# Loads of chunks 2 to 4, of x's last two groups and of the inverse table, issued from GpSimd's queue instead of SyncE's

## The chip, the cores and the metric

The kernel runs on one core of a Trainium2 chip. A core has five engines that run their own instruction streams: PE (TensorE, matrix multiplications, written as a weight load PEld and a matmul PE), DVE (VectorE), ACT (ScalarE), POOL (GpSimd) and SP (SyncE, which here only issues transfers). Sixteen DMA engines move data between the chip's memory (DRAM) and the on-chip memory; a transfer is issued by an instruction on SP, ACT or POOL and runs by itself after that. Engines wait for each other, and for transfers, through semaphores. The metric is the device time of one execution in microseconds (us), as the median of several.

## The reference

Two branches are added to the input x = A_q (2048 positions, 640 channels, bf16), both fed with the layer-normalised xn:

```python
x = A_q
xn = _layernorm(x, axis=-1)
# A: a short 4-tap shift of k, times v, a long causal convolution by FFT, gated by xn
k_shift = sum(k_pad[:, t:t + S, :] * shift_k[:, ks - 1 - t] for t in range(ks))
kv = k_shift * v
y = irfft(rfft(kv, padded to 2S) * rfft(ssm_k, padded to 2S))[:S] + kv * ssm_D
A = xn * y
# B: a gated feed-forward layer
B = (sigmoid(xn @ w_gate) * (xn @ w_up)) @ w_down
return x + A + B
```

S is 2048, the hidden size of B is 1728.

## The kernel before

Positions are laid out as 128 partitions x 16 blocks, so `x[:, b, :]` is block b of every partition.

*Branch B* goes through four groups t of four blocks each (512 positions). Group t is normalised on DVE (statistics `st` L198, `mv`, `var` L210), its `rstd` is a power on POOL (`ln_pow`, L214), `xn` is written by DVE (L219), TensorE transposes it (`pt`, L234), ACT copies it to `xnT`. Then 13 pairs of gate and up products (`pg`, `pu`, L257) follow, ACT's sigmoid, DVE's multiplication into `hT` (L272), and the down product `pd` (L301), which DVE adds to x (L306). x's group 0 is loaded at the start, groups 1 to 3 later (`load_x`, L129). The four buffers of the pool `psG` hold these products; whatever DVE or ACT has not emptied keeps TensorE back.

*Branch A* goes through five chunks c of 128 channels. Each chunk needs these loads: the taps `sraw` (`load_taps`, L143), the channel weights `dr` and the filter `hn` (`load_h`, L136 and four times L139), `kx` (a halo of two transfers, L159 and L160, and two halves, L155), and `kvh` with v (two halves, L169). ACT turns `sraw` into `sc` (`taps`, L151). DVE transposes `hn` into the second half of `kvh` (`h_turn`, L320), POOL adds `dr` to one row of it (`add_D`, L314), DVE makes kv in 16 steps (`kv_op`, L334 to L343). TensorE makes the first transform step (`ps1`, L360 and L362), ACT copies it to `t1` (L223), SP writes that to DRAM (`wr1`, L374) and reads it back in another order (`rd2`, L384); a second transform step, a product, the inverse steps with a second trip through DRAM (`wr2` L438 and L442, `rdb` L452) and the multiplication with xn follow. `t1` has two buffers: ACT's third copy waits until the first write is down. `kx` has two buffers, one for even and one for odd chunks, `kvh` has two, `hn`, `sraw`, `sc` and `dr` one each.

Tables are loaded once: `S1t` for the forward transform, `TBt` for the last inverse step (first used at 143.7 us).

The order of all work is written out by hand in the string `ORDER`: each letter takes the next step of one chain, and the program's order on every engine follows from it. `m` are the early loads in one row (weights, chunks 0 and 1, x's group 1), `n` are x's groups 2 and 3 and then `TBt`; `h`, `K`, `V` and `T` are the loads of `hn`, `kx`, `kvh` and `sraw` for the later chunks; `H`, `D` and `k` are `h_turn`, `add_D` and `kv_op`; `P` is `ln_pow`; `w` and `r` are `wr1` and `rd2`. Every engine works strictly in its own order, so an instruction that waits holds back all that stand behind it on the same engine. In the kernel before, all transfers but three at the start stand in SP's order, about 160 instructions long. Each transfer in a queue also waits, by the way semaphores are given out, for the eighth transfer before it.

Of the kernel before, what the change touches and what calls it, by code (L numbers as in the profile page):

```python
# [19 lines left out]
P = 128  # L20
NB = S // P
# [36 lines left out]
def kernel(  # L58
# [14 lines left out]
    nc = tc.nc  # L73
    xr = A_q.flatten_outer_dims().rearrange("(p b) d -> p b d", b=NB)
    kr = A_k.flatten_outer_dims().rearrange("(p b) d -> p b d", b=NB)
    vr = A_v.flatten_outer_dims().rearrange("(p b) d -> p b d", b=NB)
# [3 lines left out]
    Drow = A_ssm_D.rearrange("(o d) -> o d", o=1)  # L80

    s1bits, tbbits, smbits = _tables()
    srow = A_shift_k.rearrange("d m -> (d m)").rearrange("(o n) -> o n", o=1)
    S1d = nc.inline_tensor(s1bits, name="tabS1")
    TBd = nc.inline_tensor(tbbits, name="tabTB")
# [4 lines left out]
    dr = ctx.enter_context(tc.tile_pool(name="dr", bufs=1, space=bass.MemoryType.DRAM))  # L90
# [8 lines left out]
    TBt = res.tile([P, 2, NB, P], U16, name="TBt")  # L99
# [12 lines left out]
    kxs = [res.tile([P, NB + 3, P], BF16, name="kx%d" % i) for i in range(2)]  # L112
# [8 lines left out]
    sync = nc.sync  # L121
# [3 lines left out]
    cin = [dict() for _ in range(NC)]  # L125

    def load_x(eng, g, n=4):
        for b in range(4 * g, 4 * g + 4, n):
            eng.dma_start(x[:, b:b + n, :], xr[:, b:b + n, :])  # L129

    def load_h(c):

        d = cin[c]
        d["hn"] = cv.tile([P, 4, 512], BF16, name="hn")
        d["dr"] = cv.tile([1, P], BF16, name="dr")
        sync.dma_start(d["dr"][:, :], Drow[:, c * P:(c + 1) * P])  # L136
        for q in range(4):
            src = A_ssm_k[c * P:(c + 1) * P, 512 * q:512 * q + 512].rearrange("(k r) t -> r k t", k=4)
            sync.dma_start(d["hn"][32 * q:32 * q + 32, :, :], src)  # L139

    def load_taps(c):
        cin[c]["sraw"] = cv.tile([P, 4 * P], BF16, name="sraw")
        sync.dma_start(cin[c]["sraw"][:], srow[:, 4 * c * P:4 * (c + 1) * P].to_broadcast((P, 4 * P)))  # L143

    def taps(c):
        sc = cv.tile([P, 4, P], BF16, name="sc")
# [5 lines left out]
        cin[c]["sc"] = sc  # L152

    def load_k(c, lo, hi):
        sync.dma_start(kxs[c % 2][:, lo + 3:hi + 3, :], kr[:, lo:hi, c * P:(c + 1) * P])  # L155

    def load_halo(c):
        cs = slice(c * P, (c + 1) * P)
        sync.dma_start(kxs[c % 2][16:P, 0:3, :], kr[15:P - 1, NB - 3:NB, cs])  # L159
        sync.dma_start(kxs[c % 2][1:16, 0:3, :], kr[0:15, NB - 3:NB, cs])  # L160

    def slot(c):

        if "kvh" not in cin[c]:
            cin[c]["kvh"] = cv.tile([P, 2, NB, P], BF16, name="kvh", bufs=2)
        return cin[c]["kvh"]

    def load_v(c, lo, hi):
        sync.dma_start(slot(c)[:, 0, lo:hi, :], vr[:, lo:hi, c * P:(c + 1) * P])  # L169

    def load_w(eng, lo, hi, u):
        if u == 0:
# [345 lines left out]
    def step(k, fn, *args):  # L518
        chains[k].append((fn, args))
# [16 lines left out]
    def hs(c):  # L536
        return [(load_h, c)]

    def ks(c):
        return [(load_halo, c), (load_k, c, 0, 8), (load_k, c, 8, NB)]  # L540

    def vs(c):
        return [(load_v, c, 0, 8), (load_v, c, 8, NB)]

    for k in ((load_w, sync, 512, 768, 0),
              (load_w, sync, 512, 768, 1),
              (load_taps, 0),
              (sync.dma_start, SMt[:], SMd.ap()),
              (load_w, sync, 768, 1024, 0),
              (load_w, sync, 768, 1024, 1),  # L550
              (load_w, sync, 1024, 1280, 0),
              (load_w, sync, 1024, 1280, 1),
              (load_wd, sync, 0, 7),
              *ks(0),
              (load_w, sync, 1280, FF, 0),
              (load_w, sync, 1280, FF, 1),
              *hs(0),
              *vs(0),
              (load_wd, sync, 7, NFC),
              (sync.dma_start, S1t[:], S1d.ap()),  # L560
              *hs(1),
              (load_x, sync, 1),
              *ks(1),
              *vs(1)):
        step("m", *k)
    for k in ((load_x, sync, 2), (load_x, sync, 3), (sync.dma_start, TBt[:], TBd.ap())):
        step("n", *k)
    step("Z", taps, 0)

    for c in range(NC):  # L570
# [28 lines left out]
        if c == 0:  # L599
            continue  # L600
        step("T", load_taps, c)
        step("t", taps, c)
        if c > 1:
# [70 lines left out]
```

## Time and profile before

| | us |
|---|---|
| median of 3 runs (239.5 to 239.63) | 239.56 |
| the profiled execution | 240.16 |
| its span | 238.4 |
| PE busy | 232.6 (98%) |
| DVE busy | 190.5 (80%) |
| ACT busy | 140.9 (59%) |
| POOL busy, 24 instructions | 11.2 (5%) |

The profile is one execution. A busy time is the time in which an engine had an instruction running; issuing a transfer is not counted. In lines of the timeline the columns are: start in us, length in us, engine, line of the kernel, operation, written tile <- read tile, and at the end in brackets the idle time before it and what ended that. In the chain of work that ended last each line is a start, a length and what the time went to. A tile's own answer gives, for each line, the shortest, median and longest duration in ns and the first and last start. SPq and ACTq are the issues of transfers on SP and ACT; the length of such a line is that of the issue, not of the transfer.

### The profile page before, as it was taken

The page shows a single profiled execution, that of the slowest core. Times are in us where ns is not written, and L with a number is a line of the kernel's source. Part 1 is how long each engine was busy: PE and PEld are TensorE (multiplying, and loading weights), DVE is VectorE, ACT ScalarE, POOL GpSimd, SP SyncE. Part 2 cuts the span into 40 slices and gives each one's busy share as a digit, 9 for nine tenths or more (in the row PEclk, how much of TensorE's full clock was granted, in tenths as well). Part 3 has the DMA queues.
Part 4 walks back from the last instruction along what each step waited for, and adds up shares of the span by engine and source line. Part 5 has one row for each costly group of instructions (what it writes and reads, how often), then busy time and mean ns, then how long its engine had stood idle before and what let it go on. Part 6 is the DMA issues. An engine that isn't in the chain of part 4 may idle for free.

```text
span 238.4 us, 5555 instructions
## 1 busy us (share of the span) xinstructions
PE 232.6 (98%) x2265; PEld 134.8 (57%) x2265; DVE 190.5 (80%) x350; ACT 140.9 (59%) x178; POOL 11.2 (5%) x24
## 2 busy tenths in 40 slices
PE   8899999999999999999999999999999999999994
PEld 2664445877555555667754434577664434456772
DVE  4633989999999999999999999865585695968372
ACT  2343322728557898764888787997558858764000
POOL 5210000020000000002000000000000000000000
PEclk9999999999999999999999999999999999999999
DMA  7999999998998999998444889875849795285494
GB/s 213 291 315 236 254 326 294 197 257 236 251 312 252 259 292 292 297 252 313 154 179 143 235 237 265 216 231 202 230 119 223 186 282 126 83 241 145 123 303 137
DMA packets 89119, 54.82 MB, mean 230 GB/s; under 512 B 47814, under 2 KB 83206, under 8 KB 88838
## 3 DMA queue, kind: packets, MB, share of 16 engines
q1 hardware_dynamic: 88150, 53.66, 81.3%
q10 hardware_dynamic: 944, 0.82, 1.1%
q8 instruction: 17, 0.28, 0.5%
q14 instruction: 8, 0.07, 0.1%
HBM read 36.12 MB, written 18.35 MB: 228 GB/s over the span
## 4 chain that ended last, share of the span: by engine, by line
PE 91%; DMA 5%; ACT 2%; issue 0%; ACTq 0%; DVE 0%
PE pd L301 26%; PE pg L257 22%; PE pu L257 22%; PE psb L461 4%; PE ps L360 3%; PE ps L362 3%; PE ps L393 3%; DMA w<-in_B_w_up_dram 3%; PE psa L422 2%; PE pg L278 2%; PE pt L234 2%; DMA d<-t 2%; ACT t L223 1%; PE pu L248 1%; PE pg L248 1%
## 5 line engine op out<-in xcount | busy, mean ns | idle before, releaser
L257 PEld LDWEIGHTS <-w 128*128 128x128 bf16 x500 | 46.4, 98 | 54.4 <-issue 5.3
L301 PE MATMUL pd<-wd,hT 128*128 128x320 bf16 (+2 forms) x448 | 64.3, 299 | 0.0
L257 PE MATMUL pg<-xnT,w 128*128 128x512 bf16 x250 | 62.2, 379 | 0.0
L257 PE MATMUL pu<-xnT,w 128*128 128x512 bf16 x250 | 62.2, 379 | 0.0
L301 PEld LDWEIGHTS <-hT 128*128 128x128 bf16 x448 | 42.3, 98 | 18.5 <-issue 1.7
L266 ACT ACTIVATE sig<-pg 128x512 bf16<-128x512 f32 x52 | 31.3, 605 | 29.8 <-PE pg L257 28.0
L272 DVE TENSOR_TENSOR hT<-sig,pu 128x512 bf16<-128x512 bf16 x52 | 35.2, 680 | 15.5 <-PE pu L257 9.6
L223 ACT CAST t<-ps 128x1024 bf16<-128x1024 f32 x40 | 39.2, 1023 | 12.1 <-DMA d<-t 7.9
L223 ACT CAST xz<-ps 128x1024 bf16<-128x1024 f32 x40 | 38.5, 1017 | 10.6 <-PE ps L393 10.5
L306 DVE TENSOR_TENSOR x<-pd,x 128x320 bf16<-128x320 f32 (+2 forms) x32 | 15.3, 479 | 15.5 <-PE pd L301 15.3
L408 DVE TENSOR_TENSOR xz<-xz 128x2048 bf16<-128x2048 bf16 x20 | 24.3, 1217 | 0.2
L360 PE MATMUL ps<-kvh,S1t 128*128 128x128 bf16 x160 | 21.2, 217 | 0.5 <-ACT t L223 0.5
L362 PE MATMUL ps<-kvh,S1t 128*128 128x128 bf16 x160 | 21.2, 220 | 0.0
L340 DVE TENSOR_TENSOR acc<-acc,tmp 128x1024 bf16<-128x1024 bf16 x30 | 20.7, 689 | 0.6
L338 DVE TENSOR_TENSOR tmp<-kx,sc 128x1024 bf16<-128x1024 bf16 x30 | 20.5, 685 | 0.4
L223 ACT CAST ao<-psa 128x1024 bf16<-128x1024 f32 x16 | 15.6, 1014 | 6.0 <-PE psa L422 3.9
L362 PEld LDWEIGHTS <-S1t 128*128 128x128 bf16 x160 | 15.4, 96 | 2.9 <-issue 0.8
L466 DVE TENSOR_TENSOR yx<-psb,xn 128x512 bf16<-128x512 f32 x20 | 13.8, 690 | 3.9 <-PE psb L461 2.9
L360 PEld LDWEIGHTS <-S1t 128*128 128x128 bf16 x160 | 15.5, 97 | 2.3
L223 ACT COPY xnT<-pt 128x640 bf16<-128x640 bf16 x16 | 10.2, 708 | 10.9 <-PE pt L234 10.6
L198 DVE BATCH_NORM_STATS2 st<-x 128x6 f32<-128x320 bf16 x32 | 13.7, 470 | 2.6 <-DMA x<-in_A_q_dram 2.6
L406 DVE STREAM_SHUFFLE xz<-xz 128x512 f32<-128x512 f32 x20 | 14.5, 725 | 0.0
(44 smaller groups left out, 147.5 us busy)
## 6 DMA issues: line engine op xcount, KB each, us to landing
d<-t SPq DMA_DIRECT2D x20, 512.0 KB, 3.9
t<-d SPq DMA_DIRECT2D x20, 512.0 KB, 5.2
bi<-d SPq DMA_DIRECT2D x8, 512.0 KB, 5.2
d<-ao SPq DMA_DIRECT2D x6, 512.0 KB, 4.1
kx<-in_A_k_dram SPq DMA_DIRECT2D x10, 256.0 KB, 5.1
hn<-in_A_ssm_k_dram SPq DMA_DIRECT2D x20, 128.0 KB, 5.9
kvh<-in_A_v_dram SPq DMA_DIRECT2D x10, 256.0 KB, 5.3
x<-in_A_q_dram SPq DMA_DIRECT2D x3, 640.0 KB
```

The source lines that it names most:

```text
L223: nc.scalar.copy(out=out, in_=in_)
L257: nc.tensor.matmul(pg[:, :], lhsT=w[:, c, u * UP + fc * P:u * UP + (fc + 1) * P], rhs=xnT[:, :, c, :], start=(c == 0), stop=(c == NC - 1))
L266: nc.scalar.activation(sig[fc][:, :], pgs[0, fc][:, :], ACT.Sigmoid)
L272: nc.vector.tensor_tensor(hT[:, fc, :], sig[fc][:, :], pgs[1, fc][:, :], ALU.mult)
L301: nc.tensor.matmul(pd[:, :], lhsT=hT[:, fc, bb * P:(bb + 1) * P], rhs=wd[:, fc, es], start=(fc == 0), stop=(fc == NFC - 1))
L306: nc.vector.tensor_tensor(x[:, 4 * t + bb, es], pds[bb, half][:, :], x[:, 4 * t + bb, es], ALU.add)
L338: nc.vector.tensor_tensor(d["tmp"][:, :, :], kx[:, lo + 3 - m:hi + 3 - m, :], sb(m), ALU.mult)
L340: nc.vector.tensor_tensor(d["acc"][:, :, :], d["acc"][:, :, :], d["tmp"][:, :, :], ALU.add)
L360: nc.tensor.matmul(ps[:, i, 0:P], lhsT=S1[:, b, h, :], rhs=cin[c]["kvh"][:, 0, b, :], start=True, stop=True)
L362: nc.tensor.matmul(ps[:, i, P:2 * P], lhsT=S1[:, b, h, :], rhs=hp[:, b // 2, b % 2, :], start=True, stop=True)
L406: nc.vector.stream_shuffle(z[:, 2, :, :].bitcast(F32), z[:, 1, :, :].bitcast(F32), swap)
L408: nc.vector.tensor_tensor(z[:, 1:3, :, :], z[:, 0:1, :, :].to_broadcast((P, 2, 8, P)), z[:, 1:3, :, :], ALU.mult)
```

## The change

The loads of `dr`, `hn`, `sraw`, `kx` (halo and halves) and `kvh` take their queue from a new function: GpSimd for chunks 2, 3 and 4, SP for chunks 0 and 1. The three loads of chain `n` (x's groups 2 and 3, `TBt`) are issued by GpSimd too. `ORDER` is untouched, so these 39 issues keep their places in the program's order; they now stand in POOL's order, between its `add_D` and `ln_pow`, instead of in SP's. What stands on PE and DVE, and in which order, is the same.

```diff
+    def queue(c):
+        return nc.gpsimd if c > 1 else sync
+
     def load_h(c):
...
-        sync.dma_start(d["dr"][:, :], Drow[:, c * P:(c + 1) * P])
+        queue(c).dma_start(d["dr"][:, :], Drow[:, c * P:(c + 1) * P])
         for q in range(4):
             src = A_ssm_k[c * P:(c + 1) * P, 512 * q:512 * q + 512].rearrange("(k r) t -> r k t", k=4)
-            sync.dma_start(d["hn"][32 * q:32 * q + 32, :, :], src)
+            queue(c).dma_start(d["hn"][32 * q:32 * q + 32, :, :], src)
     def load_taps(c):
...
-        sync.dma_start(cin[c]["sraw"][:], srow[:, 4 * c * P:4 * (c + 1) * P].to_broadcast((P, 4 * P)))
+        queue(c).dma_start(cin[c]["sraw"][:], srow[:, 4 * c * P:4 * (c + 1) * P].to_broadcast((P, 4 * P)))
     def load_k(c, lo, hi):
-        sync.dma_start(kxs[c % 2][:, lo + 3:hi + 3, :], kr[:, lo:hi, c * P:(c + 1) * P])
+        queue(c).dma_start(kxs[c % 2][:, lo + 3:hi + 3, :], kr[:, lo:hi, c * P:(c + 1) * P])
     def load_halo(c):
         cs = slice(c * P, (c + 1) * P)
-        sync.dma_start(kxs[c % 2][16:P, 0:3, :], kr[15:P - 1, NB - 3:NB, cs])
-        sync.dma_start(kxs[c % 2][1:16, 0:3, :], kr[0:15, NB - 3:NB, cs])
+        queue(c).dma_start(kxs[c % 2][16:P, 0:3, :], kr[15:P - 1, NB - 3:NB, cs])
+        queue(c).dma_start(kxs[c % 2][1:16, 0:3, :], kr[0:15, NB - 3:NB, cs])
     def load_v(c, lo, hi):
-        sync.dma_start(slot(c)[:, 0, lo:hi, :], vr[:, lo:hi, c * P:(c + 1) * P])
+        queue(c).dma_start(slot(c)[:, 0, lo:hi, :], vr[:, lo:hi, c * P:(c + 1) * P])
...
-    for k in ((load_x, sync, 2), (load_x, sync, 3), (sync.dma_start, TBt[:], TBd.ap())):
+    for k in ((load_x, nc.gpsimd, 2), (load_x, nc.gpsimd, 3), (nc.gpsimd.dma_start, TBt[:], TBd.ap())):
         step("n", *k)
```

## The prediction

> **What bounds the kernel now.** I read the page's first part and its chain, then the table by stage, the waits, and last, in order of time, the queues of SP, POOL, DVE and PE between 40 and 120 us, where all the moved loads lie.
>
> The page's first part, for the whole span:
>
> ```profile
> PE 232.6 (98%) x2265; PEld 134.8 (57%) x2265; DVE 190.5 (80%) x350; ACT 140.9 (59%) x178; POOL 11.2 (5%) x24
> ```
>
> TensorE leaves 238.4 - 232.6 = 5.8 us. The table by stage says where, and where none is left (columns: stretch and length; busy us of PE, PEld, DVE, ACT, POOL with instructions; clock; DMA share; GB/s):
>
> ```profile
> 40.00:50.00 10.00, 10.00 (x103) 7.96 (x102) 9.77 (x21) 4.63 (x6) 0.43 (x1) 1.00 0.92 209
> 50.00:60.00 10.00, 10.00 (x95) 7.60 (x93) 9.86 (x20) 6.15 (x8) 1.75 (x2) 1.00 0.90 269
> 60.00:70.00 10.00, 10.00 (x62) 5.06 (x60) 9.74 (x17) 4.89 (x7) 0.00 (x0) 1.00 1.07 273
> 70.00:80.00 10.00, 9.51 (x93) 6.15 (x91) 9.51 (x15) 8.35 (x11) 0.42 (x1) 1.00 0.99 260
> 80.00:90.00 10.00, 10.00 (x93) 4.95 (x92) 9.86 (x18) 8.90 (x12) 0.00 (x0) 1.00 0.93 281
> 90.00:100.00 10.00, 10.00 (x102) 5.67 (x101) 9.63 (x15) 7.74 (x10) 0.42 (x1) 1.00 1.03 299
> 100.00:110.00 10.00, 10.00 (x110) 6.85 (x108) 9.73 (x26) 5.78 (x6) 1.10 (x1) 1.00 0.88 251
> ```
>
> TensorE is full in every stretch but one, which lacks 0.49 us. VectorE is nearly full as well, and so are the 16 DMA engines (0.88 to 1.07). POOL alone is free. The rest of the 5.8 us lies at the two ends, which the moved loads do not touch. The 0.49 us stands in the chain like this (start, us, what):
>
> ```profile
> 70.56 1.93 ACT t L223 x2
> 72.50 3.88 DMA d<-t
> 76.48 1.02 ACT t L223
> ...
> 77.55 0.22 PE ps L360
> ```
>
> A write of the first transform's output takes 3.88 us, ScalarE needs its buffer back, and TensorE waits for ScalarE. So the most that any change to the loads between 40 and 120 us can win is about 0.5 us, or 0.2%; losses have no such lid.
>
> **Part 1: what leaves SP.** 39 issues leave it: 12 for each of chunks 2 to 4 (dr 1, hn 4, sraw 1, kx 4, kvh 2), two of x, and TBt. Added from their rows in SP's timeline this is 23.6 us of issuing. It wins only where a write or read of the transform stood ready behind it. Two such places: the write at 46.23 (its copy ended about 45.66, from the row "43.74 2.87 ACT L223 x3"; SP was then waiting at sraw for ACT's sc) and the one at 49.22 (copy ended 48.02). The first can go 0.5 us earlier, the second 1.1; the write at 72.50 left 0.01 us after its copy and gains nothing from SP. Off the path: 0.
>
> **Part 2: what POOL gets.** The same 39 issues, in the same relative order, between its own add_D (L314) and rstd power (L214). Their price there is in no row. For a small one (dr, hn, sraw) the floor is SP's quickest issue, 0.26 us, the ceiling POOL's longest instruction of its own, 1.39 us; I take 1.0, nearer POOL's rows, since that engine does the work. For a quarter-megabyte kx or kvh load, 1,024 rows of 256 bytes, the nearest row is that load on SP (L155, min/median/max):
>
> ```profile
> L155 SPq DMA_DIRECT2D kx<-in_A_k_dram x10: 385/430/3021, 15.1 to 90.1; - x10
> ```
>
> Floor 0.39, ceiling 3.02, the latter from a queue that was backed up; I take the middle, 1.7. The Trainium skill, page "DMA: Bandwidth & Descriptors", section "Latency and other measured facts", puts the first byte of a load at about 1 us from GpSimd and 0.6 from SP; by that alone each load would land 0.4 us later, and the sum below would keep its sign.
>
> **Part 3: do the loads still land in time?** They wait for the same freed buffers as before, so they cannot start much earlier: sraw(3) and sraw(4) for ScalarE's sc (67.2, 84.8), with kx and kvh behind them; kvh(3) and kvh(4) for TensorE (about 75.9, 93.0), with add_D, x and rstd behind. Each load also waits for the eighth before it on its queue, long down at these prices. The question is POOL's backlog. These rows carry it, first POOL, then SP, VectorE and TensorE:
>
> ```profile
> 51.16 1.32 POOL L214 TENSOR_TENSOR rstd<-var,mhalf 128x4 f32<-128x4 f32 x1 [5.45 <-DVE var L210]
> 94.57 0.42 POOL L314 TENSOR_TENSOR kvh<-kvh,dr 1x128 bf16<-1x128 bf16 x1 [15.98 <-DVE kvh L320]
> ```
>
> ```profile
> 47.06 2.05 SPq L139 DMA_DIRECT2D hn<-in_A_ssm_k_dram  x4
> 93.10 1.13 SPq L169 DMA_DIRECT2D kvh<-in_A_v_dram  x2
> 96.23 0.42 SPq L129 DMA_DIRECT2D x<-in_A_q_dram  x1
> ```
>
> ```profile
> 56.40 2.10 DVE L320 STREAM_TRANSPOSE kvh<-hn 128x512 f32<-128x512 f32 x2
> 103.89 0.88 DVE L198 BATCH_NORM_STATS2 st<-x 128x6 f32<-128x320 bf16 x2
> 110.34 1.51 DVE L219 TENSOR_SCALAR xn<-x,mv,rstd 128x640 bf16<-128x640 bf16 x4
> ```
>
> ```profile
> 111.33 0.84 PE pt L234 x15
> ```
>
> *rstd of x's group 1.* It now stands behind dr(2) and hn(2)'s four loads, free when VectorE ends hn(1) at 46.2. At 1.0 each they end by 50.7, 0.4 us before rstd could start at 51.16: hidden. At the ceiling of 1.39 they end at 52.7, 1.5 late, and xn at 52.53 waits.
>
> *hn(2)* landed before at about 49.1 + 6.2 = 55.3; now 50.7 + 5.2 = 55.9 against 56.40: hidden, thinly. The kx and kvh loads of chunks 2 to 4 have 4 to 25 us until VectorE reads them (75.13 for kx(2)'s second half is the nearest).
>
> *x's group 2* is the pinch. Before: issued at 96.23; the longest landing of an x load is 7.0 us, so down at 103.2, used at 103.89. Now it stands behind both kvh(4) loads (buffer free at about 93.0) and add_D(4): 93.0 + 2 x 1.7 + 0.42 = 96.8, 0.6 us later, and with 0.4 for the dearer issue it is down at 104.2. VectorE stalls 0.3. TensorE's transposes begin at 111.33 with the first xn ready at 110.34 + 0.44 = 110.78: 0.55 us of cover, so 0 on the path. The cover is gone when the kvh load costs more than about 1.85 us.
>
> *x's group 3 and TBt* now wait behind the rstd of group 2 (done 110.3) instead of going at 107.0 and 107.6; used at 124.59 and 143.7: 0. *add_D(2 to 4)* wait behind kvh loads; TensorE reads their result 15 us later or more: 0.
>
> **Part 4: sharing.** With DMA at 0.9 to 1.07, what used to queue behind a write now runs beside it. At 46 us hn(2), 512 KB, stood behind the write of 46.23; at 209 GB/s it takes 2.5 us, and if half passes ahead the write lands 1.25 later, less the 0.5 of part 1: +0.75. ScalarE's copy at 52.75 waits for it; TensorE's next two groups, at 54.25 and 54.99, had 0.53 and 0.31 us in hand: +0.4. At 72.5 the write of 3.88 us shares with kx(3), issued on POOL at about 70 to 73.5 instead of by 70.8; half of 256 KB at 260 GB/s is 0.5: the wait of 0.49 becomes 1.0. Bounds: the first could cost nothing, the second could vanish (-0.49), or both take whole loads (+1.6, +1.0).
>
> **Sum.** 0 + 0 + 0 + 0.4 + 0.5 = +0.9 us. The profiled execution took 240.16 us (span 238.4), 0.6 above the median of 239.56; as a step it goes on the median: 240.5.
>
> **The rivals.**
>
> *The load generator is the bound.* Between the rstd at 52.5 and x's group 2 POOL issues 18 small and 12 large loads: 18 x 1.0 + 12 x 1.7 + 1.3 = 40 us of 44. It fits only up to about 2.0 us a large load; at 2.4 x's group 2 starts some 4 us late, TensorE has 0.55 of that: 239.56 + 4 + 0.9, about 244.5. At the ceilings it would be over 255. Against it: POOL's own rows are 0.42 to 1.39 us.
>
> *VectorE locks POOL out.* Both engines read and write the same memory; if POOL could write its load lists only while VectorE is idle, it would have 2 us of the 70 in the table above. Even if that only doubled every price, 18 x 2.0 + 12 x 3.4 = 77 us would have to fit in 44, and x's group 2 comes 33 us late: about 270. Against it: add_D took 0.42 us at 94.57 and rstd 1.32 at 51.16 with VectorE at 9.6 to 9.9 of 10 us. The Trainium skill, page "SBUF — State Buffer", sections "SBUF: two separate sides" and "Who interferes with whom", states this lock for vector instructions that use both ports, and says that a two-input tensor_tensor takes only the read side. By that narrower form only xn's 1.51 us at 52.53 and 110.34 would hold POOL, with nothing urgent behind, and the sum stays.
>
> *All hidden.* hn(2) does not overtake, or the later groups have more in hand: 239.6.
>
> *Faster.* The write of 72.50 has the queue to itself and lands 0.5 us sooner: TensorE's gap closes, 239.1. It decides only if kx(3) is already down by then. This is all there is to win.
>
> **Chances.** Small loss 0.42 (own range 240.1 to 242), load generator 0.17, lock 0.03, hidden 0.31, faster 0.07. 0.2% is 0.48 us, about what a measurement here can tell from no change: faster 0.07, same 0.31, slower 0.62. The range leaves out the little beyond -0.49 below and the upper half of the load generator's case with the lock above: 239.1 to 245.5.
>
> **What would show it.** Right: POOL's load rows near 1 us and 1.7 us; VectorE's statistics at 103.9 pushed by less than 1 us; ScalarE's copies at 52.75 and 76.48 later; TensorE's gap near 77 about 1 us. Wrong: kx rows on POOL above 2 us (the first rival) or under 1 us with the writes no longer than 3.9 us (hidden or faster).

## The result, and the profile after

The changed kernel takes 241.46 us (median of 4 runs, 241.27 to 241.92), the kernel before 239.59 beside it: a ratio of 1.0082, 95% interval [1.0064, 1.0099], 1.9 us slower. The profiled execution took 241.92 us with a span of 239.8 (before 240.16 and 238.4). One execution of experiment 4 (1,350 us) and one of experiment 10 (842 us, the one that was profiled) were disturbed and count in no median or ratio below. Lines of the changed kernel stand three lower in the file: L374 is now L377, L223 is L226, and so on.

First the page's first part and its packet counts, of the changed kernel:

```profile
PE 232.8 (97%) x2264; PEld 135.0 (56%) x2265; DVE 190.6 (79%) x350; ACT 141.1 (59%) x178; POOL 37.9 (16%) x63
...
DMA packets 75253, 54.82 MB, mean 229 GB/s; under 512 B 34479, under 2 KB 68044, under 8 KB 74972
...
q1 hardware_dynamic: 71836, 45.89, 67.9%
q0 software_dynamic: 2448, 7.77, 12.0%
```

TensorE's work is nearly the same, 232.8 us against 232.6; it is idle for 239.8 - 232.8 = 7.0 us instead of 5.8. POOL is busy 26.7 us longer, for 39 loads. The same bytes travel, 7.77 MB of them now from POOL's queue (q0; q1 is SP's).

The table by stage, with the columns of the one before (the stretches from 40 to 70 and from 100 to 200 us are full in both):

```profile
70.00:80.00 10.00, 9.98 (x94) 6.38 (x92) 9.83 (x15) 8.94 (x11) 4.45 (x7) 1.00 0.80 238
80.00:90.00 10.00, 10.00 (x94) 4.92 (x93) 9.86 (x17) 8.90 (x13) 5.30 (x9) 1.00 0.96 291
90.00:100.00 10.00, 8.34 (x86) 4.43 (x85) 7.79 (x12) 5.92 (x8) 2.73 (x4) 1.00 1.00 295
```

TensorE loses 1.66 us between 90 and 100 us, where it had been full, and 0.02 at 77 us, where it had lost 0.49. The two profiled executions differ by 1.76 us: 1.2 are this idle time, 0.2 are TensorE's own work, and about 0.4 lie outside the span. The chain of work that ended last shows what it waited for, and ScalarE's, SP's and TensorE's timelines show the links:

```profile
94.73 1.09 PE pu L260 x5
...
95.88 0.07 ACT t L226
95.95 0.84 issue
96.79 1.03 ACT t L226
97.82 0.04 issue
97.86 0.65 PE psa L425 x30
```

```profile
89.22 2.78 SPq L377 DMA_DIRECT2D d<-t  x2
```

```profile
90.62 1.01 ACT L226 CAST t<-ps 128x1024 bf16<-128x1024 f32 x1
91.70 0.60 ACT L269 ACTIVATE sig<-pg 128x512 bf16<-128x512 f32 x1
95.88 1.93 ACT L226 CAST t<-ps 128x1024 bf16<-128x1024 f32 x2 [3.58 <-PE pu L260]
```

```profile
96.94 0.39 PE L425 MATMUL psa<-xz,SMt 32*32 32x512 bf16 x2 [1.13 <-ACT t L226]
97.86 0.65 PE L425 MATMUL psa<-xz,SMt 32*32 32x512 bf16 x30 [0.53 <-ACT t L226]
```

ScalarE made two copies of chunk 3's first transform step (each copy is two CAST instructions, one for each half), then had to wait 3.58 us for the third. The bracket names TensorE's `pu`, but that product had nothing to do with the copy; the copy needs one of the two `t` buffers, and the first buffer is free when the write issued at 89.22 is down. The trace's semaphore records have the last part of that write complete at 95.78, 0.10 us before the copy starts. TensorE's `psa` in turn waited 1.13 and 0.53 us for the output buffers that the two halves of the third copy empty: the 1.66 us.

The same place before the change, in ScalarE's, SP's and TensorE's timelines of the kernel before:

```profile
93.89 1.93 ACT L223 CAST t<-ps 128x1024 bf16<-128x1024 f32 x2 [1.09 <-DMA d<-t]
```

```profile
85.44 2.11 SPq L143 DMA_DIRECT2D sraw<-in_A_shift_k_dram  x1
...
88.65 0.39 SPq L155 DMA_DIRECT2D kx<-in_A_k_dram  x1
89.71 0.35 SPq L374 DMA_DIRECT2D d<-t  x1
90.11 0.42 SPq L155 DMA_DIRECT2D kx<-in_A_k_dram  x1
```

```profile
96.24 0.65 PE L422 MATMUL psa<-xz,SMt 32*32 32x512 bf16 x32
```

From issue of the write to the third copy it took 93.89 - 89.71 = 4.18 us (the write was complete at 93.79); after the change, 95.88 - 89.22 = 6.66. ScalarE's wait of 1.09 us was covered then: TensorE's `psa` began at 96.24 without a stall. POOL's timeline of the changed kernel shows what is new ahead of the write:

```profile
84.61 0.56 POOL L146 DMA_DIRECT2D sraw<-in_A_shift_k_dram  x1 [2.97 <-ACT sc L154]
85.17 0.72 POOL L162 DMA_DIRECT2D kx<-in_A_k_dram  x1
85.88 0.59 POOL L163 DMA_DIRECT2D kx<-in_A_k_dram  x1
86.47 1.81 POOL L158 DMA_DIRECT2D kx<-in_A_k_dram  x2
```

Before, one half of chunk 4's `kx` was issued 1.06 us ahead of the write and the other 0.40 behind it. Now both halves, 512 KB, are issued between 86.5 and 88.3, ahead of it, because POOL is not held up by SP's 2.11 us issue of `sraw` and by the reads in front of that. VectorE does not need chunk 4's `kx` before 116 us.

### The profile page after: what moved, and what is told of

It is laid out like the page before. It is cut to its first block, busy times and chain, and to the rows that moved or that the text cites. A ratio compares the mean times of both kernels' runs of the same rounds, so it can differ in the third digit from the quotient of the medians.

```text
span 239.8 us, 5565 instructions
## 1 busy us (share of the span) xinstructions
PE 232.8 (97%) x2264; PEld 135.0 (56%) x2265; DVE 190.6 (79%) x350; ACT 141.1 (59%) x178; POOL 37.9 (16%) x63
## 3 DMA queue, kind: packets, MB, share of 16 engines
q0 software_dynamic: 2448, 7.77, 12.0%
## 4 chain that ended last, share of the span: by engine, by line
PE 90%; DVE 3%; DMA 3%; ACT 1%; issue 1%; ACTq 0%; DVEq 0%
PE pd L304 26%; PE pu L260 22%; PE pg L260 22%; PE psb L464 4%; PE ps L363 3%; PE ps L365 3%; PE ps L396 3%; DMA w<-in_B_w_up_dram 3%; PE psa L425 2%; PE pg L281 2%; PE pt L237 2%; DVE tmp L341 1%; PE pu L251 1%; PE pg L251 1%; DVE hT L275 1%
## 5 line engine op out<-in xcount | busy, mean ns | idle before, releaser
L226 ACT CAST t<-ps 128x1024 bf16<-128x1024 f32 x40 | 39.2, 1025 | 12.7 <-PE ps L365 4.6
L226 ACT CAST xz<-ps 128x1024 bf16<-128x1024 f32 x40 | 38.5, 1018 | 10.6 <-PE ps L396 10.5
L226 ACT CAST ao<-psa 128x1024 bf16<-128x1024 f32 x16 | 15.6, 1014 | 5.2 <-PE psa L425 3.1
L226 ACT COPY xnT<-pt 128x640 bf16<-128x640 bf16 x16 | 10.2, 703 | 11.9 <-PE pt L237 11.6
```

What stands on the lines that cost most here:

```text
L226: nc.scalar.copy(out=out, in_=in_)
```

## Theories

*The main one:* chunk 4's `kx` now stands whole ahead of the write of 89.2 us, because its second half overtakes that write; the write lands some 2.5 us later on the shared DMA engines, and about 1.7 us of that reaches TensorE. *Rivals:* a fixed price of using POOL's queue at all; a price spread over all moved loads; large packets from POOL starving the smaller ones of SP's transfers; and the order of the bytes alone, whatever the queue.

All experiments were timed in several rounds against the kernel before, whose median in them was 239.66 to 239.81 us. "Lag" is the time from the issue of chunk 3's first write to the start of ScalarE's third copy.

## Experiment 1: chunk 4 back on SP

```diff
     def queue(c):
-        return nc.gpsimd if c > 1 else sync
+        return nc.gpsimd if c in (2, 3) else sync
```

> The changed kernel with all twelve loads of chunk 4 back on SP; chunks 2 and 3, x's two groups and the inverse table stay on POOL. Crowding theory (chunk 4's loads, issued by POOL between 84.6 and 88.3 us, run beside the read back of the transform, and the write of 89.22 that queues behind that read lands 6.6 us after its issue): TensorE's loss of 1.66 us between 90 and 100 us goes, the gap near 77 us stays closed, so 241.5 - 1.7 = 239.8 us or a little less. Rival, a price of the POOL queue itself (setting up, ends, or every load a little): 27 of 39 loads remain, so the time stays above 240.7 us.

Measured: 239.98 us, 1.0001 [0.9985, 1.0017]. The lag is 93.78 - 89.78 = 4.00 us, TensorE full again:

```profile
90.00:100.00 10.00, 10.00 (x102) 5.61 (x100) 9.70 (x15) 7.81 (x10) 0.96 (x2) 1.00 0.98 261
```

Without chunk 4's, the loads of chunks 2 and 3, of x and of the inverse table show no cost on POOL (the interval ends at 0.17%). The loss needs chunk 4's loads.

## Experiment 2: only chunk 4's `kx` halves back on SP

```diff
     def load_k(c, lo, hi):
-        queue(c).dma_start(kxs[c % 2][:, lo + 3:hi + 3, :], kr[:, lo:hi, c * P:(c + 1) * P])
+        (sync if c == 4 else queue(c)).dma_start(kxs[c % 2][:, lo + 3:hi + 3, :], kr[:, lo:hi, c * P:(c + 1) * P])
```

> The changed kernel with only the two quarter-megabyte kx loads of chunk 4 back on SP, where they stand around the write of 89 us as they did before. Crowding theory with kx(4) as the culprit: the same as with the whole chunk back, 239.6 to 239.9 us, TensorE full between 90 and 100 us. If hn(4), sraw(4), the halo or kvh(4) do it: no more than half of the 1.66 us returns, above 240.5 us. Price of the queue itself: 241.3 us or more.

Measured: 240.52 us, 1.0037 [1.0013, 1.0061]; lag 94.40 - 89.79 = 4.61 us, TensorE full from 90 to 100 in the profiled execution. About half of the loss is gone (0.37% is left of 0.71 to 0.82%), where the expectation of the main theory was all of it. In this execution TensorE loses nothing between 90 and 100 us, so the trace does not show where the rest goes.

## Experiment 3: the kernel before, with only chunk 4's `sraw` and `kx` on POOL

The edit to the kernel before, for `sraw`, both halo transfers and the `kx` halves alike:

```diff
-        sync.dma_start(kxs[c % 2][:, lo + 3:hi + 3, :], kr[:, lo:hi, c * P:(c + 1) * P])
+        (nc.gpsimd if c == 4 else sync).dma_start(kxs[c % 2][:, lo + 3:hi + 3, :], kr[:, lo:hi, c * P:(c + 1) * P])
```

> The kernel before with only chunk 4's sraw, halo and kx loads (five) on POOL. Crowding theory: they go at about 85 to 88 us beside the read back, the first write of chunk 3 lands late by 1.5 to 2.5 us, TensorE loses 1 to 2 us between 90 and 100 us and keeps its 0.5 us gap near 77: 240.6 to 241.6 us. If the loss needs the other chunks' loads too (all of the queue shifted): 239.6 us. Price of the queue itself: at most a few tenths above 239.6 us.

Measured: 240.44 us, 1.0026 [1.0011, 1.0041]; lag 94.59 - 89.43 = 5.16 us, TensorE 9.77 of 10. These five loads alone bring a loss, but about a third of it: something else among the moved loads adds to it.

## Experiment 4: the kernel before, with one load on POOL

```diff
-        sync.dma_start(d["dr"][:, :], Drow[:, c * P:(c + 1) * P])
+        (nc.gpsimd if c == 2 else sync).dma_start(d["dr"][:, :], Drow[:, c * P:(c + 1) * P])
```

> The kernel before with one 256-byte load, chunk 2's dr, on POOL and nothing else. It measures what using POOL's queue at all costs outside the work. The profiled times before and after leave 1.8 and about 2.0 us outside the span. Crowding theory: within 0.2 us of the kernel before. A fixed price of the queue: 0.3 to 0.5 us more, found in the time outside the span or at its ends, which would explain that much of the 1.9 us.

Measured: 239.83 us, 1.0001 [0.9986, 1.0016]; lag 4.07 us. No fixed price for using POOL's queue shows; the interval leaves room for 0.16%, or 0.4 us.

## Experiment 5: the changed kernel again

No edit; it gives the changed kernel's numbers on the chip and in the rounds of the next three.

> The changed kernel unaltered, as the standard for the three that follow on the same chip, and a second profile of it: is the late write the same in another execution? All theories: 241.0 to 241.6 us, 0.7 to 0.85% over the kernel before; crowding theory: the first write of chunk 3, issued at about 89 us, lands 5.5 us or more later and TensorE lacks 1 to 2 us between 90 and 100 us. Chance theory (the profile caught a rare delay and the loss is spread elsewhere): that stretch is full.

Measured: 241.36 us, 1.0071 [1.0041, 1.0101]; lag 96.27 - 90.31 = 5.96 us, TensorE 9.05 of 10 from 90 to 100 us, and 9.39 from 70 to 80. So the loss repeats at 90 to 100; the gap near 77 us does not tell the kernels apart: it was 0.49 before, 0.02 and 0.61 in two executions of the changed kernel, and 0 in experiments 3 and 8, which are the kernel before up to that point.

## Experiment 6: chunk 4's `kx` on POOL, but behind the write

The three K steps of chunk 4 (halo, two halves) move in `ORDER` to just behind x's group 2:

```diff
-    apKgKswAkaugAkaKkwsakgVHAVgAuDHgswkcugCkgkskCgnuWakaAkgAkgukwbguBrlgBlgulbgBrlgBuglkPpgnulgllleenuEe
+    apgswAkaugAkakwsakgVHAVgAuDHgswkcugCkgkskCgnKKKuWakaAkgAkgukwbguBrlgBlgulbgBrlgBuglkPpgnulgllleenuEe
```

> The changed kernel with chunk 4's halo and both kx loads moved in POOL's own order to behind x's group 2, so that they are issued at about 96 us instead of 85.2 to 88.3; VectorE reads them at 116. All 39 loads still go through POOL. Crowding theory: the write of 89 us lands within 4.5 us, TensorE is full between 90 and 100 us, and the time is that of the kernel before within 0.3% (239.6 to 240.4 us on this chip), unless the loads now crowd the next write or read at 102 to 105 us. Any theory in which POOL's queue or its software loads cost by themselves: no better than the changed kernel.

Measured: 240.16 us, 1.0009 [0.9996, 1.0022]. POOL's timeline of this kernel shows the halves well behind the write (SP issues that at 89.33), ScalarE's shows the copy:

```profile
97.02 1.82 POOL L158 DMA_DIRECT2D kx<-in_A_k_dram  x2
```

```profile
93.81 1.93 ACT L226 CAST t<-ps 128x1024 bf16<-128x1024 f32 x2 [1.39 <-PE pu L260]
```

The lag is 4.48 us and TensorE full. Every load is still on POOL, with its packets and its price; only the time of three steps differs, and nearly all of the loss is gone. This is the run that carries the cause: chunk 4's `kx`, halo and halves, ahead of the write.

## Experiment 7: the reads of the transform on POOL as well

If POOL's large packets starved small ones, the write's neighbours in SP's queue, the 512-byte reads of `rd2`, would gain from going by POOL too:

```diff
-        sync.dma_start(t2[:, :, :], src[8 * s4:8 * s4 + 8].rearrange("r p e -> p r e"))
+        (nc.gpsimd if s in (2, 3) else sync).dma_start(t2[:, :, :], src[8 * s4:8 * s4 + 8].rearrange("r p e -> p r e"))
```

> The changed kernel with, in addition, the two reads back of chunk 0 at 82 to 85 us (512 KB each, 512-byte packets on SP's queue) issued by POOL, in front of sraw(4) and kx(4). kx(4) stays on POOL at its early place. Small-packet theory (a read in packets of 512 bytes gets one turn in two against packets of 4,096 and so an eighth of the bytes, and the write behind it in SP's queue has to wait): the read is packed too, the write of 89 us has SP's queue to itself and lands within 4.5 us, TensorE keeps its time between 90 and 100 us, 239.6 to 240.4 us. Bytes theory (what counts is only how many bytes stand before the write on the 16 engines): the bytes are the same and all go ahead, no gain, 241 us or more.

Measured: 241.73 us, 1.0077 [1.0056, 1.0097]; lag 96.71 - 90.45 = 6.26 us. The queue's line on the page shows that they went that way, 1.05 MB more:

```profile
q0 software_dynamic: 2736, 8.82, 13.9%
```

Nothing is won, so the size of the reads' packets is not the cause. The run is no test of when `kx` goes: behind the two reads on POOL its halves were issued at 88.72 and 89.64, about 2.2 us later than in the changed kernel, the second one only 0.81 us before the write. The reads, issued at 83.36 and 85.99, stood ahead of the write as well.

## Experiment 8: the same order within SP's queue

The kernel before, all loads on SP; in `ORDER` the second half of chunk 4's `kx` moves ahead of the write:

```diff
-    apKgKswAkaugAkaKkwsakgVHAVgAuDHgswkcugCkgkskCgnuWakaAkgAkgukwbguBrlgBlgulbgBrlgBuglkPpgnulgllleenuEe
+    apKgKKswAkaugAkakwsakgVHAVgAuDHgswkcugCkgkskCgnuWakaAkgAkgukwbguBrlgBlgulbgBrlgBuglkPpgnulgllleenuEe
```

> The kernel before, all on SP, with the second half of kx(4) issued before the write of 89.7 us instead of behind it. Bytes theory: 256 KB more ahead of the write delay its landing by about 1.0 us (256 KB at 260 GB/s) to 5.2 us, ScalarE's third copy ends about 0.6 us beyond TensorE's cover of 0.45: 0.3 to 0.7 us slower than before. Small-packet theory: in one queue the order is kept and the write waits only for those 1.0 us; the same 0.3 to 0.7 us, clearly less than the 1.7 us of the changed kernel. Within 0.1 us of before: the loads ahead of the write are no part of the cause.

Measured: 240.82 us, 1.0033 [1.0017, 1.0050]. SP's timeline of this kernel, then ScalarE's and TensorE's:

```profile
88.63 1.34 SPq L155 DMA_DIRECT2D kx<-in_A_k_dram  x2
90.06 2.47 SPq L374 DMA_DIRECT2D d<-t  x2
```

```profile
94.98 1.93 ACT L223 CAST t<-ps 128x1024 bf16<-128x1024 f32 x2 [2.15 <-DMA d<-t]
```

```profile
96.96 0.65 PE L422 MATMUL psa<-xz,SMt 32*32 32x512 bf16 x30 [0.30 <-ACT t L223]
```

With no load on POOL, 256 KB put ahead of the write make the lag 4.92 us, and TensorE waits at `psa` for ScalarE just as in the changed kernel. Here the profile puts ScalarE's wait down to the write by name. So the mechanism needs nothing of POOL's queue; a load ahead of the write is enough. It is smaller here, however: TensorE lacks 0.30 us between 90 and 100 us, while 0.33% is 0.8 us, so the trace of this one execution shows less than half of the loss. Whether POOL's queue adds something of its own is not settled by this run.

## Experiments 9 and 10: what makes up the rest

Both ran on another chip than the experiments above. Experiment 9 is the changed kernel with chunk 4's `dr` and `hn` on SP (the line for `dr` changes in the same way):

```diff
-            queue(c).dma_start(d["hn"][32 * q:32 * q + 32, :, :], src)
+            (sync if c == 4 else queue(c)).dma_start(d["hn"][32 * q:32 * q + 32, :, :], src)
```

> The changed kernel with chunk 4's filter loads (four hn and dr, POOL at 79 to 82 us) back on SP at their old place in front of the write of 82 us; everything else stays on POOL, kx(4) early. Bytes theory (the loss is what kx(4), the halo and sraw put ahead of the write of 89 us): hn(4) was ahead of it in both orders, nothing changes, 0.6 to 0.85% over the kernel before. Two-queue theory (the read back at 82 to 85 us is thinned by hn(4) and so still runs when kx(4) comes, and one slow engine holds the write up): the read ends by 91 us, the write lands within 5.3 us, 0.2 to 0.45% over the kernel before.

Measured: 240.59 us, 1.0053 [1.0031, 1.0076]; lag 94.81 - 89.82 = 4.99 us, TensorE 9.96 of 10 in the profiled execution.

Experiment 10 is the changed kernel with the second half of chunk 4's `kx` on SP, where it stands behind the write again:

```diff
-        queue(c).dma_start(kxs[c % 2][:, lo + 3:hi + 3, :], kr[:, lo:hi, c * P:(c + 1) * P])
+        (sync if c == 4 and lo else queue(c)).dma_start(kxs[c % 2][:, lo + 3:hi + 3, :], kr[:, lo:hi, c * P:(c + 1) * P])
```

> The changed kernel with only the second half of kx(4), 256 KB, back on SP behind the write of 89 us, its old place. Bytes theory: the write has those 256 KB less ahead of it and lands 1 us sooner, 4.7 to 5.3 us after its issue; the gain is what the same 256 KB cost in the kernel before, 0.33% with an interval of 0.17 to 0.5%, so 0.3 to 0.55% over the kernel before remain. Two-queue theory: the halo, sraw and first half still run beside the read on POOL's queue, the write stays 5.5 us or later, at least 0.6% over.

Measured: 240.91 us, 1.0052 [1.0036, 1.0069]; there is no lag for it.

Both ratios lie between that of the kernel before and those of the changed one, but their intervals overlap the changed kernel's, so the times alone do not show that either wins a part back. Experiment 9's ratio falls between what its two theories expected; its lag and its reads, which end at 90.4 us, are as the two-queue theory expected. Experiment 10's ratio is in the range of the bytes theory, and its interval reaches into that of the other. In order of lag the runs read:

| kernel | lag, us | ratio |
|---|---|---|
| chunk 4 on SP (1) | 4.00 | 1.0001 |
| `dr` of chunk 2 alone on POOL (4) | 4.07 | 1.0001 |
| before | 4.18 | 1 |
| `kx` of chunk 4 behind the write (6) | 4.48 | 1.0009 |
| `kx` halves of chunk 4 on SP (2) | 4.61 | 1.0037 |
| all on SP, half of `kx` ahead (8) | 4.92 | 1.0033 |
| `hn` of chunk 4 on SP (9) | 4.99 | 1.0053 |
| `sraw` and `kx` of chunk 4 alone on POOL (3) | 5.16 | 1.0026 |
| changed, again (5) | 5.96 | 1.0071 |
| reads on POOL too (7) | 6.26 | 1.0077 |
| changed | 6.66 | 1.0082 |

A lag is one execution's and a ratio a median's, so neighbours may change places; but over the table they go together roughly. With up to about 4.5 us of lag the time is that of before. This fits the cover in the kernel before: the two halves of ScalarE's third copy, from 93.89 on, ended at 93.89 + 1.93 = 95.82, TensorE was busy with products until `psa` began at 96.24, so there were 0.42 us in hand.

What stays open is how the 0.8% divide. The intervals of experiments 2, 3, 8, 9 and 10 overlap, and in the profiled executions TensorE lacks 0, 0.23, 0.30 and 0.04 us between 90 and 100 us in experiments 2, 3, 8 and 9, against 0.6 to 1.3 us by their ratios. The executions of experiment 9 range from 239.97 to 242.58 us, so one profiled execution need not stand for the median.

By the trace's packet records, SP's 512-byte reads issued from 82 us on end at 90.3 us before and at 94.0 after (92.5 in experiment 5, 90.5 in 3). In the changed kernel the last 76 of their 2,048 packets end after 90.5, some of them beside the write, whose own packets start at 91.5. With `hn` on SP they end at 90.4 (experiment 9), with `kx` behind the write at 91.9 (experiment 6). This fits that `hn` and `kx` of chunk 4 both delay them, in one execution each; late reads alone do not make the loss, since experiment 6 has them without it. Part of the lag is a straggler: the last two of the 16 completions of the write of 89.22 came 0.81 us behind the other fourteen (0.18 in the kernel before, 0.59 in experiment 5). Which of these weighs how much was not told apart.

## Why the prediction was right, and where it was not

**Direction and size.** Slower by a few tenths of a per cent by sharing of the DMA engines was the forecast of 240.5 us; it was 241.46, inside the whole range and inside the likeliest case's own range of 240.1 to 242. The sum was +0.9 and the runs say +1.9. That the figure came out is in part luck: neither of the two places whose terms made up the +0.9 lost anything beyond its own variation, and the place that lost 1.66 us was not in the sum. Of the four signs that the prediction gave for being right, none came as described: POOL's loads cost about half, VectorE's statistics were pushed by 1.53 us and not by less than 1, ScalarE's two copies came earlier in that profile and not later, and the gap near 77 us was 0.02 and 0.61 us and not about 1.

**Part 1** (SP loses 23.6 us of issuing, worth 0). Right. The write at 46.23 went at 45.91, and ScalarE's copies at 52.75 came 1.85 us *earlier*, at 50.90. Nothing was won by that; TensorE was full there in both.

**Part 2** (1.0 us a small load, 1.7 a large one). About twice too high. POOL's timeline of the changed kernel:

```profile
46.76 2.24 POOL L142 DMA_DIRECT2D hn<-in_A_ssm_k_dram  x4 [0.25 <-DMA kx<-in_A_k_dram]
51.06 1.41 POOL L217 TENSOR_TENSOR rstd<-var,mhalf 128x4 f32<-128x4 f32 x1 [2.06 <-DVE var L213]
...
92.87 1.75 POOL L172 DMA_DIRECT2D kvh<-in_A_v_dram  x2 [4.60 <-PE ps L365]
...
95.03 0.59 POOL L129 DMA_DIRECT2D x<-in_A_q_dram  x1
```

A small load is 2.24 / 4 = 0.56 us, a large one about 0.9; both lie between the bounds given, nearer to the floor. The 0.4 us by which a load from POOL was to land later does not show either: from issue to landing the medians are 5.0 us for `kx`, 4.7 for `kvh` and 5.7 for `hn`, against 5.1, 5.3 and 5.9 from SP before (over more chunks, so this is no fine comparison). The low prices took away the *load generator* rival: 26.7 us of POOL for all 39 loads, where 40 had been reckoned for 30 of them and 1.3 us of POOL's own work.

**Part 3** (do they land in time). Right that all are hidden, wrong on the pinch. `rstd` of group 1 started at 51.06, 0.10 earlier than before, VectorE's turn of chunk 2's `hn` at 56.41 against 56.40. x's group 2 was expected 0.6 us later than 96.23 and went at 95.03, *earlier* by 1.2; down 5.9 us later, it was there 4.5 us before VectorE came to it at 105.42. VectorE's 1.53 us delay there comes from the late copy, not from x: VectorE had waited 2.05 us at 96.3 for a `sig` that stands behind that copy on ScalarE.

The sentence of part 3 that failed is "they cannot start much earlier". For chunk 4's `kx` it is wrong: the buffer was free and `sraw` went at 84.61, but in SP's order 3.00 us of reads and then the 2.11 us issue of `sraw` stood in front. Free of those, `kx` went about 2 us earlier, and past the write.

**Part 4** (sharing). The term of the sum that decided: right in kind, since sharing cost time, but wrong in place and size. It was looked for where ScalarE waited longest, at 46 us (+0.4) and 72.5 us (+0.5). Both measured nothing. At 46 us `hn` of chunk 2 did not pass ahead: POOL issued it at 46.76, still behind the write, which went at 45.91, and TensorE was full from 40 to 70 us. At 72.5 us both halves of chunk 3's `kx` had been ahead of the write before the change too (issued from 69.36, and from 69.35 after); the copy of 76.48 came at 75.99, with a gap that varies by itself (experiment 5). The loss came at 89 us, where before ScalarE waited only 1.09 us and TensorE not at all: 1.66 us. What would have shown it were SP's three rows at 88.65, 89.71 and 90.11: a half of `kx` ahead of the write and one behind, neither of them urgent. "The most that any change can win is about 0.5; losses have no such lid" held.

**Rivals.** *VectorE locks POOL out:* not so. The Trainium skill, page "SBUF — State Buffer", sections "SBUF: two separate sides" and "Who interferes with whom", states the lock for vector instructions in a mode that uses both ports, and for those with two inputs only against a GpSimd instruction that reads the memory. With VectorE over 9.8 of 10 us busy between 70 and 90, POOL's loads took 0.53 to 0.93 us each, so a lock by any busy VectorE is out. VectorE's `xn`, the instruction that the prediction took for the narrower form, ran from 52.52 to 54.04, and the two halo issues that POOL made from 52.45 to 53.81 took 0.76 and 0.60 us, against 0.72 and 0.57 to 0.59 elsewhere: no hold shows there. Whether another vector instruction would lock POOL out these rows don't decide. *Faster* by a write at 72.5 that has the queue to itself: the gap did close in the profiled execution, but it opens again in experiment 5. *All hidden* would have been right without chunk 4 (experiment 1), or with its `kx` behind the write (experiment 6). No variant was measured faster than the kernel before.

The Trainium skill, page "DMA: Bandwidth & Descriptors", section "Issuing engines are not separate DMA queues", says that transfers from any engine end up on the same 16 DMA engines and interleave, and that a second issuing engine saves only the time of issuing. The runs agree: the same rate of 229 GB/s over the span with two queues as 230 with one, 23.6 us of issuing off SP worth nothing, and a write whose buffer comes back after 6.66 us instead of 4.18.

## What to carry to other kernels

A queue with much in it is also an order: moving loads out of it lets them start as soon as their buffers are free, and where the DMA engines are as full as here (0.96 to 1.00 between 80 and 100 us), loads that are not urgent can then stand ahead of a write that somebody waits for. Before moving loads, list for each write on the path what stands just behind it in the queue and what holds back the loads in front of it, and keep those loads behind the write by their place in the program (experiment 6: 0.09% instead of 0.8%, no clear difference from the kernel before). Look also at waits that are covered now, with the cover in us beside them, not only at the ones that show on the critical chain.

## What was not expected of the hardware

- POOL's queue merges rows. By the packet records a `kx` half of 1,024 rows of 256 bytes is sent in packets of 4,096 bytes, where SP sends packets of 256; all loads of q0 average 7.77 MB / 2,448 = 3.2 KB, and the packets of the whole kernel fall from 89,119 to 75,253. The rate did not rise, 229 GB/s against 230.
- POOL issues 1,024 rows in 0.9 us and 128 rows in 0.56, so rows cost it little. On SP, issues of the same `kx` load had taken 0.39 to 3.02 us, with a median of 0.43.
- The bytes that change places do not account for the whole lag. One half of `kx` ahead of the write instead of behind it, within SP's queue, made the lag 4.92 - 4.18 = 0.74 us longer, and 256 KB at that kernel's 278 GB/s between 90 and 100 us are 0.9 us. In the changed kernel the same half passed the write, other loads of chunk 4 went earlier with it, and the lag grew by 1.8 to 2.5 us in two executions; the reads and the straggling completions named above are what the trace shows of the rest.
